# FFT filter and gated FFN on one core: three float32r passes in one first stage, another order of table loads, and matmuls on a cleared tile at the start

## The chip, the cores and the metric

The kernel runs on one core of one Trainium2 chip. The metric is device microseconds of that core for one execution, the median of several. The engines have short names in the profile: PE (TensorE matmul), PEld (its weight load), DVE (VectorE), ACT (ScalarE), POOL (GpSimd) and SP (SyncE, which here only issues DMAs).

## The reference

For 8 batches of 3136 rows by 256 columns, `x` is filtered in the frequency domain along its rows, and a gated feed-forward network with a depthwise convolution of three rows follows:

```python
X = np.fft.rfft(x, axis=1)
y = np.fft.irfft(X * (filt_r + 1j * filt_i)[None], n=x.shape[1], axis=1).astype(np.float32)
h = np.maximum(y @ w_in, 0.0)                       # 256 -> 1024
conv_out[s] = sum(conv_w[k] * h[s + k - 1] for k in range(3))
out = (h * sigmoid(conv_out)) @ w_out               # 1024 -> 256
```

## The kernel before, in words

The FFT of length 3136 = 112 x 28 is done as matmuls with tables. A batch is cut into 14 tiles of [112, 2, 256]; a tile goes through these steps, each named by its function:

- `load` (SP queue) brings a tile of `x` from DRAM.
- `first` is the first stage: float32 products of `x` with the 112x112 table `s1_sb`. For batches 0, 1, 3 and 5 it makes four products of 112 columns with the result turned (line 335), and `keep` copies them on ACT to the buffer `turn`; there are two of these. For batches 2, 4, 6 and 7 (`THROUGH_DRAM`) it makes two products of 256 columns (line 330), `keep` copies them on ACT to `ao` (line 341) and an ACT-queue DMA stores them to `a_dram`.
- The tile comes back in the other layout: `turn` (PE transposes, line 357) and `turned_rows` (an ACT copy to `a`, line 362), or `load_rows` (a DMA from `a_dram`).
- `second` (line 369) multiplies by the table `s2_sb` into `pp`. `filt` multiplies by the filter: three DVE products `u`, `v`, `v` that read `pp` in PSUM and a filter table in SBUF (lines 378 to 380), and one POOL sum `z` = `u` + `v` in SBUF (line 382).
- `third` (line 230) multiplies `z` by `i1_sb`, and `store` copies the result on ACT to `sb` (line 234) and stores it to `b_dram` by a DMA on the ACT queue.

A turn of the loop over i issues one step for each of several tiles: the first stage of tile i - 1, and, with m = i - 17, `second` of m - 1, `filt` of m - 2, `third` of m - 4. So a turn has `third`, `first`, `second` and perhaps `turn` on PE in that order. The order on each engine is that in which the code is written (`manual_schedule`). I call turns whose `first` belongs to batches 2, 4, 6, 7 *DRAM turns*, and those of batches 0, 1, 3, 5 *turned turns*. In turns whose tile m is of batches 0, 1, 3, 5 PE transposes too ("with transposes").

Two kinds of work run beside it. The tables `s2_sb`, `i1_sb` and the filter tables `t1_sb`, `t2_sb` come in seven pieces by POOL-queue DMAs (`load_filter`, at the turns of `FILTER_AT`; a small POOL copy `pace` holds each back until ACT has copied the tile before). The weights, stored as float64, are converted in eight slabs by a generator, `convert_weights`, from which each turn takes one step, or two: seven steps of a slab are DVE instructions on 128x512 words (`to_f32`, lines 150 to 162, behind the three products of the turn), the other three are a POOL sum, two ACT roundings to float32r and two POOL differences. Before, this runs from turn 36 at one step a turn, and two where i is a multiple of 8.

Then the FFN runs over 28 chunks of 896 rows. Its products are float32r, each in three passes on high and low parts (`mm3`, lines 167 to 169): the high part is the value rounded to float32r (`hi_act`), the low part what is left.

Of the kernel before, what the change touches and what calls it, by code (L numbers as in the profile page):

```python
# [19 lines left out]
G = 28  # L20
# [96 lines left out]
def tile_fft_filter_gated_ffn(  # L117
# [122 lines left out]
    xp = forward_pools.enter_context(tc.tile_pool(name="xp", bufs=1, side="right"))  # L240
    s1_sb = xp.tile([112, 112], F32, name="s1_sb")
    with (
        tc.tile_pool(name="fc", bufs=1) as fc,
# [23 lines left out]

        def load_filter(n, kept):
            b, k = kept
            nc.gpsimd.tensor_copy(pace, turns[turned_by[b] % 2][0:1, 0, 2 * k, 0:1])  # L270
            sl = slice(4 * n, 4 * n + 4)
            if n < 7:
                nc.gpsimd.dma_start(out=s2_sb[:, sl], in_=s2[:, sl])
                nc.gpsimd.dma_start(out=t2_sb[0:56, sl], in_=fi[0:56, sl])
                nc.gpsimd.dma_start(out=t1_sb[64:120, sl], in_=fr[64:120, sl])
            if n == 6:
                nc.gpsimd.dma_start(out=t1_sb[0:56, sl], in_=fr[0:56, sl])
            if n:
                sl = slice(4 * n - 4, 4 * n)
                nc.gpsimd.dma_start(out=i1_sb[:, sl], in_=i1[:, sl])  # L280

# [8 lines left out]
        def load_weights(k):  # L290
            raws[k] = raw = cv.tile([128, 2, 512], I32, name="raw")
            nc.sync.dma_start(out=raw, in_=w.rearrange("p (k t n) -> p k t n", t=2, n=512)[:, k])
# [6 lines left out]
        def convert_weights():  # L299

            for k in range(8):
                raw = raws.pop(k)
                em = cv.tile([128, 2, 512], I32, name="em", bufs=1)
                ws = cv.tile([128, 2, 256], F32, name="ws", bufs=1)
                yield from to_f32(ws.rearrange("p t n -> p (t n)"), raw.rearrange("p t n -> p (t n)"), em[:, 0], em[:, 1])
# [12 lines left out]

        def load(b, p):
            r = xp.tile([112, 2, D], F32, name="x", bufs=XBUFS)  # L320
            nc.sync.dma_start(out=r, in_=x[b].rearrange("(p n) d -> p n d", n=N2)[:, 2 * p:2 * p + 2])
            rows["x", b, p] = r

        def first(b, p):

            r = rows.pop(("x", b, p))
            if b in THROUGH_DRAM:
                ps = fps.tile([112, 2, D], F32, name="ps")
                for j in range(2):
                    nc.tensor.matmul(ps[:, j], lhsT=s1_sb, rhs=r[:, j], start=True, stop=True)  # L330
                return ps
# [55 lines left out]

        XBUFS = 6
# [10 lines left out]
        for i in range(XBUFS):  # L399
            load_first(i)  # L400
        csteps, wsteps = convert_conv(), convert_weights()
        done = NP * B + 1
        NI = done + LATE + N2 // 2 + 2
        END = NP * B - 4
        with tc.manual_schedule(engines=COMPUTE | {mybir.EngineType.SP}):
            for i in range(NI):
                m = i - SKEW
                if i == done:
# [3 lines left out]
                    yps.append(ctx.enter_context(tc.tile_pool(name="y_even", bufs=1, side="right", reuse_waits="tile")))  # L412
                if i:
                    load_first(i + XBUFS - 1)
                if i == 8:
# [26 lines left out]
                if pf is not None:  # L442
                    keep(*at(i - 1), pf)
                if i in FILTER_AT:
                    load_filter(FILTER_AT.index(i), at(i - 1))
                if pa is not None:
                    turned_rows(*at(m), pa)
                if 0 <= m - 1 < NP:
                    copy_filter(m - 1)
                if 14 <= i < 22:  # L450
# [125 lines left out]

THROUGH_DRAM = (2, 4, 6, 7)
PLAG = 6
PAUSE = (8,)
# [45 lines left out]
```

## Time and profile before

| what | value |
|---|---|
| median of 3 runs | 1535.78 us (1534.64 to 1537.65) |
| profiled execution, its time / its span | 1534.63 us / 1532.9 us |
| mean granted clock | 0.998 of full |
| PE busy in the span | 1511.3 us (99%) |
| DVE / ACT / POOL busy | 1285.1 / 1220.3 / 731.9 us |
| the loop's turns 29 to 112 (first stages of batches 2 to 7) | from 63.49 to 306.60 us |
| the FFN after the loop | from about 350 us |

The span is that of the profiled execution, and 1.7 us lie around it. Busy time says how long an engine had an instruction in it, not that the others waited for it; what sets the pace of a stretch is read from the distance of like instructions in order of time, and from what ended the idle time before them.

### The profile page before, as it was taken

The page shows a single profiled execution, that of the slowest core. Times are in us where ns is not written, and L with a number is a line of the kernel's source. Part 1 is how long each engine was busy: PE and PEld are TensorE (multiplying, and loading weights), DVE is VectorE, ACT ScalarE, POOL GpSimd, SP SyncE. Part 2 cuts the span into 40 slices and gives each one's busy share as a digit, 9 for nine tenths or more (in the row PEclk, how much of TensorE's full clock was granted, in tenths as well). Part 3 has the DMA queues.
Part 4 walks back from the last instruction along what each step waited for, and adds up shares of the span by engine and source line. Part 5 has one row for each costly group of instructions (what it writes and reads, how often), then busy time and mean ns, then how long its engine had stood idle before and what let it go on. Part 6 is the DMA issues. An engine that isn't in the chain of part 4 may idle for free.

```text
span 1532.9 us, 27503 instructions
## 1 busy us (share of the span) xinstructions
PE 1511.3 (99%) x10080; PEld 1420.1 (93%) x10080; DVE 1285.1 (84%) x1968; ACT 1220.3 (80%) x2227; POOL 731.9 (48%) x671
## 2 busy tenths in 40 slices
PE   7999999999999999999999999999999999999998
PEld 7888888888999999999999999999999999999998
DVE  2689898888888888888888888888888888888886
ACT  4664645567888888888888888888888888888886
POOL 5555566575444444444444444444444444444444
PEclk9999999999999999999999999999999999999999
DMA  8978797982111011111101111111011111000001
GB/s 219 274 238 287 235 285 244 317 254 76 52 55 37 25 43 55 43 49 49 49 31 43 49 48 32 55 49 43 25 55 49 49 44 54 19 25 25 25 25 49
DMA packets 105670, 141.07 MB, mean 92 GB/s; under 512 B 8813, under 2 KB 71773, under 8 KB 105536
## 3 DMA queue, kind: packets, MB, share of 16 engines
q1 hardware_dynamic: 76048, 95.01, 19.8%
q10 hardware_dynamic: 27392, 37.86, 8.1%
q0 software_dynamic: 2096, 6.45, 1.6%
q8 instruction: 80, 1.31, 0.3%
q14 instruction: 54, 0.44, 0.1%
HBM read 75.06 MB, written 64.23 MB: 91 GB/s over the span
## 4 chain that ended last, share of the span: by engine, by line
PE 94%; DMA 2%; ACT 1%; POOL 1%; DVE 1%; issue 1%; SPq 0%; ACTq 0%; POOLq 0%; DVEq 0%
PE ps_h L168 12%; PE ps_h L169 12%; PE po L520 12%; PE ps_h L167 12%; PE po L522 12%; PE po L521 12%; PE ps_h L207 6%; PE ps L230 5%; PE pp L369 5%; PE ps L330 3%; PE ps L335 3%; PE ps L357 1%; DMA i_sb<-in_i 1%; POOL z L382 1%; PE ps L207 1%
## 5 line engine op out<-in xcount | busy, mean ns | idle before, releaser
L142 POOL TENSOR_TENSOR g<-t,g 128x448 fp32r<-128x448 f32 x448 | 517.8, 1156 | 652.5 <-ACT g L136 258.0
L520 PE MATMUL po<-wo,g 128*128 128x256 f32 x1568 | 441.4, 281 | 0.0
L522 PE MATMUL po<-wo,g 128*128 128x256 f32 x1568 | 433.9, 277 | 0.0
L521 PE MATMUL po<-wo,g 128*128 128x256 f32 x1568 | 433.4, 276 | 0.0
L494 DVE SCALAR_TENSOR_TENSOR t<-ps_h,cw,t 128x448 f32<-128x448 f32 x448 | 305.9, 683 | 79.2 <-ACT t L489 67.9
L167 PE MATMUL ps_h<-y,wi 128*128 128x450 f32 x896 | 328.1, 366 | 1.3 <-DVE t L500 1.3
L168 PE MATMUL ps_h<-y,wi 128*128 128x450 f32 x896 | 328.8, 367 | 0.0
L169 PE MATMUL ps_h<-y,wi 128*128 128x450 f32 x896 | 328.2, 366 | 0.0
L495 DVE SCALAR_TENSOR_TENSOR t<-ps_h,cw,t 128x448 f32<-128x448 f32 x448 | 306.5, 684 | 16.0
L489 ACT ACTIVATE t<-ps_h,cw 128x448 f32<-128x448 f32 x448 | 285.4, 637 | 41.5 <-ACT ps_h L487 0.4
L520 PEld LDWEIGHTS po<-wo,g 128*128 128x128 f32 x1568 | 294.8, 188 | 7.1
L521 PEld LDWEIGHTS po<-wo,g 128*128 128x128 f32 x1568 | 294.3, 188 | 5.7
L522 PEld LDWEIGHTS po<-wo,g 128*128 128x128 f32 x1568 | 294.5, 188 | 0.2 <-POOL g L142 0.2
L500 DVE TENSOR_TENSOR t<-ps_h,t 128x448 f32<-128x448 f32 x448 | 275.4, 615 | 0.1
L487 ACT ACTIVATE ps_h<-ps_h 128x450 f32<-128x450 f32 x448 | 251.9, 562 | 26.6 <-PE ps_h L169 22.0
L499 ACT ACTIVATE t<-t 128x448 f32<-128x448 f32 x448 | 255.1, 569 | 14.2 <-DVE t L495 12.4
L136 ACT ACTIVATE g<-t 128x448 fp32r<-128x448 f32 x448 | 254.7, 568 | 0.2 <-DVE t L500 0.2
L382 POOL TENSOR_TENSOR z<-u,v 120x512 f32<-120x512 f32 x112 | 156.8, 1401 | 125.9 <-DVE v L380 97.1
L169 PEld LDWEIGHTS ps_h<-y,wi 128*128 128x128 f32 x896 | 167.9, 187 | 14.0
L167 PEld LDWEIGHTS ps_h<-y,wi 128*128 128x128 f32 x896 | 169.6, 189 | 8.4 <-DVE t L500 1.8
L168 PEld LDWEIGHTS ps_h<-y,wi 128*128 128x128 f32 x896 | 167.9, 187 | 6.7
L139 DVE TENSOR_TENSOR y<-ps_h,y 128x448 fp32r<-128x448 f32 x98 | 103.7, 1058 | 71.1 <-ACT y L136 71.1
(69 smaller groups left out, 1616.1 us busy)
## 6 DMA issues: line engine op xcount, KB each, us to landing
x<-in_x SPq DMA_DIRECT2D x112, 224.0 KB, 3.6
b_dram<-sb ACTq DMA_DIRECT2D x109, 224.0 KB, 3.5
out<-ot SPq DMA_DIRECT2D x27, 896.0 KB, 4.1
br<-b_dram SPq DMA_DIRECT2D x98, 224.0 KB, 2.6
a_dram<-ao ACTq DMA_DIRECT2D x56, 224.0 KB, 3.2
a<-a_dram SPq DMA_DIRECT2D x56, 224.0 KB, 4.1
raw<-in_w SPq DMA_DIRECT2D x8, 512.0 KB, 5.5
turn<-b_dram SPq DMA_DIRECT2D x14, 224.0 KB, 4.7
```

What stands on the lines that cost most here:

```text
L142: nc.gpsimd.tensor_tensor(out=dst, in0=src, in1=hi.bitcast(F32), op=ALU.subtract)
L167: nc.tensor.matmul(ps, lhsT=wh, rhs=rh, start=start, stop=False, **kw)
L168: nc.tensor.matmul(ps, lhsT=wh, rhs=rl, start=False, stop=False, **kw)
L169: nc.tensor.matmul(ps, lhsT=wl, rhs=rh, start=False, stop=stop, **kw)
L489: nc.scalar.activation(t, h[:, 1:SUB + 1], AF.Copy, scale=cw[:, 1, f:f + 1])
L494: nc.vector.scalar_tensor_tensor(out=t, in0=h[:, 0:SUB], scalar=cw[:, 0, f:f + 1], in1=t, op0=ALU.mult, op1=ALU.add)
L495: nc.vector.scalar_tensor_tensor(out=t, in0=h[:, 2:SUB + 2], scalar=cw[:, 2, f:f + 1], in1=t, op0=ALU.mult, op1=ALU.add)
L499: nc.scalar.activation(t, t, AF.Sigmoid)
L500: nc.vector.tensor_mul(t, h[:, 1:SUB + 1], t)
L520: nc.tensor.matmul(o, lhsT=gh[:, sl], rhs=wo[0][:, f], start=first, stop=False, skip_group_check=True)
L521: nc.tensor.matmul(o, lhsT=gh[:, sl], rhs=wo[1][:, f], start=False, stop=False, skip_group_check=True)
L522: nc.tensor.matmul(o, lhsT=gl[:, sl], rhs=wo[0][:, f], start=False, stop=last, skip_group_check=True)
```

## The change

Three things are changed, all before the FFN.

1. In DRAM turns the first stage becomes three float32r passes over the 512 columns of a tile: `s1` and `x` are split into high and low parts. In each such turn this adds one ACT instruction (`split_high`, 512 columns), one POOL difference (384 columns) ahead of the sum `z`, and one DVE difference (`BY_DVE` = 128 columns) behind the three products of `filt`. Two float32 products of 256 columns go, three float32r products of 512 come. There are 56 such turns.
2. The steps of the weight conversion are dealt out by a credit from turn 32 on: 0.75 a DRAM turn, 1.5 a turned turn. Only one raw slab is held, and the next is loaded when the slab before is through its DVE steps. Buffers for `x` go from 6 to 4 after the first 18 tiles; the first 18 lie in the part of `t2_sb` that is filled last.
3. The tables come in the order of `TABLES` (turns for `s2`, the filter and `i1` of each piece). DVE clears `eye_sb`, and 12 products of 128 columns on it stand ahead of PE's first product.

```diff
+    s1_parts = [xp.tile([112, 112], F32R, name=f"s1{h}") for h in range(2)]
...
-            raws[k] = raw = cv.tile([128, 2, 512], I32, name="raw")
+            raws[k] = raw = cv.tile([128, 2, 512], I32, name="raw", bufs=1)
...
+                if k < 7:
+                    load_weights(k + 1)
...
-                if k < 6:
-                    load_weights(k + 2)
...
-            r = xp.tile([112, 2, D], F32, name="x", bufs=XBUFS)
+            n = b * NP + p
+            if n < AHEAD * 3:
+                at = 2 * (n % AHEAD) + G - 2 - 2 * AHEAD
+                r = t2_sb[0:112, at:at + 2]
+            else:
+                r = xp.tile([112, 2, D], F32, name="x", bufs=4)
...
+        def split_high(b, p):
+            h = xp.tile([112, 2, D], F32R, name="xh", bufs=2)
+            hi_act(h, rows["x", b, p])
+            rows["xh", b, p] = h
+
+        def split_low(b, p):
+            r, h = rows["x", b, p], rows["xh", b, p]
+            t = xp.tile([112, 2, D], F32R, name="xl", bufs=2)
+            r, h, lo = (t.rearrange("p n d -> p (n d)") for t in (r, h, t))
+            rows["xl", b, p] = t
+            sl = slice(BY_DVE, 2 * D)
+            lo_pool(lo[:, sl], r[:, sl], h[:, sl])
+            yield
+            sl = slice(0, BY_DVE)
+            lo_dve(lo[:, sl], r[:, sl], h[:, sl])
...
-                for j in range(2):
-                    nc.tensor.matmul(ps[:, j], lhsT=s1_sb, rhs=r[:, j], start=True, stop=True)
+                mm3(ps, *s1_parts, rows.pop(("xh", b, p)), rows.pop(("xl", b, p)))
...
-        FILTER_AT = (12, 15, 18, 20, 22, 24, 26, 28)
...
+            for k in range(WARM):
+                nc.tensor.matmul(pw[:, 0:128], lhsT=eye_sb, rhs=eye_sb, start=True, stop=True)
...
+                low = iter(())
+                if (bp := at(i)) and bp[0] in THROUGH_DRAM:
+                    split_high(*bp)
+                    low = split_low(*bp)
+                next(low, None)
                 if bp := at(m - 2):
                     filt(*bp)
+                next(low, None)
...
-                if i in (28, 34):
-                    load_weights((i - 28) // 6)
-                if i >= 36:
-                    for _ in range(2 if i % 8 == 0 else 1):
+                if i == 28:
+                    load_weights(0)
+                if i >= 32:
+                    credit += 0.75 if (bp := at(i)) and bp[0] in THROUGH_DRAM else 1.5
+                    for _ in range(int(credit)):
+                        credit -= 1
                         next(wsteps, None)
...
+TABLES = (
+    (0, 9, 11, 14),
+    (1, 13, 15, 17),
...
+WARM = 12
+BY_DVE = 128
+AHEAD = 6
```

Three engines' orders follow, at the places that matter. `v_105` to `v_108` are the two buffers of `v`, `em`, `ws` and `raw` the conversion's words, `xh` and `xl` the high and low part of a tile of `x`.

DVE in DRAM turns of batch 4, before: the three products of a turn, and behind them at most a conversion step.

```order
L378 TENSOR_TENSOR u<-pp,t_sb 120x512
L379 TENSOR_TENSOR v_105<-pp,t_sb 56x512
L380 TENSOR_TENSOR v_105<-pp,t_sb 56x512
L156 TENSOR_SCALAR em<-raw 128x512
L378 TENSOR_TENSOR u<-pp,t_sb 120x512
L379 TENSOR_TENSOR v_106<-pp,t_sb 56x512
L380 TENSOR_TENSOR v_106<-pp,t_sb 56x512
L158 SCALAR_TENSOR_TENSOR ws<-em 128x512
```

And DVE in DRAM turns of batch 4 of the changed kernel:

```order
L400 TENSOR_TENSOR u<-pp,t_sb 120x512
L401 TENSOR_TENSOR v_108<-pp,t_sb 56x512
L402 TENSOR_TENSOR v_108<-pp,t_sb 56x512
L139 TENSOR_TENSOR xl<-x,xh 112x128
L152 TENSOR_SCALAR em<-raw 128x512
L400 TENSOR_TENSOR u<-pp,t_sb 120x512
L401 TENSOR_TENSOR v_107<-pp,t_sb 56x512
L402 TENSOR_TENSOR v_107<-pp,t_sb 56x512
L139 TENSOR_TENSOR xl<-x,xh 112x128
L154 TENSOR_TENSOR em<-em 128x512
```

The low part stands between the products and the conversion step, so a turn has two instructions on SBUF operands alone where it had one. Counted over the whole order, seven turns of each of the batches 2, 4, 6 and 7 have both.

DVE in turned turns of batch 3 of the changed kernel, where the credit deals out two steps every other turn:

```order
L400 TENSOR_TENSOR u<-pp,t_sb 120x512
L401 TENSOR_TENSOR v_107<-pp,t_sb 56x512
L402 TENSOR_TENSOR v_107<-pp,t_sb 56x512
L154 TENSOR_TENSOR em<-em 128x512
L400 TENSOR_TENSOR u<-pp,t_sb 120x512
L401 TENSOR_TENSOR v_108<-pp,t_sb 56x512
L402 TENSOR_TENSOR v_108<-pp,t_sb 56x512
L156 TENSOR_SCALAR em<-raw 128x512
L158 SCALAR_TENSOR_TENSOR em<-em 128x512
```

Two DVE steps stand together in four turns of batch 3 and in four of batch 5; before, there were five such turns in the whole loop.

ACT in a DRAM turn with transposes, before (`DMA` rows are issues on its queue):

```order
L234 ACTIVATE sb<-ps 112x512
L236 DMA b_dram_62<-sb 112x512
L341 ACTIVATE ao<-ps 112x512
L342 DMA a_dram_57<-ao 112x2x256
L362 ACTIVATE a<-ps 112x512
```

ACT in such a turn of the changed kernel:

```order
L136 ACTIVATE xh<-x 112x512
L234 ACTIVATE sb<-ps 112x512
L236 DMA b_dram_62<-sb 112x512
L363 ACTIVATE ao<-ps 112x512
L364 DMA a_dram_57<-ao 112x2x256
L384 ACTIVATE a<-ps 112x512
```

The rounding of the next tile's high part stands between `a` of one turn and `sb` of the next; nothing else of ACT's turn moved.

POOL's first table loads, before:

```order
L270 COPY pace<-turn_102 1x1
L273 DMA s_sb<-in_s 112x480
L274 DMA t_sb<-in_fi 56x1024
L275 DMA t_sb<-in_fr 56x1024
L270 COPY pace<-turn_101 1x1
L273 DMA s_sb<-in_s 112x480
L274 DMA t_sb<-in_fi 56x1024
L275 DMA t_sb<-in_fr 56x1024
L280 DMA i_sb<-in_i 120x448
```

And those of the changed kernel:

```order
L271 COPY pace<-turn_104 1x1
L275 DMA s_sb<-in_s 112x480
L271 COPY pace<-turn_104 1x1
L279 DMA t_sb<-in_fi 56x1024
L280 DMA t_sb<-in_fr 56x1024
L271 COPY pace<-turn_104 1x1
L275 DMA s_sb<-in_s 112x480
L271 COPY pace<-turn_104 1x1
L277 DMA i_sb<-in_i 120x448
L271 COPY pace<-turn_103 1x1
L279 DMA t_sb<-in_fi 56x1024
L280 DMA t_sb<-in_fr 56x1024
```

The first piece of `i1` (`i_sb`) stood behind two pieces of the filter; now it stands behind one, and the first load is asked for at turn 9 and no longer at turn 12.

## Rows read from the trace of the kernel before

**Rows 1.** The page's chain that ended last, by engine.

```profile
PE 94%; DMA 2%; ACT 1%; POOL 1%; DVE 1%; issue 1%; SPq 0%; ACTq 0%; POOLq 0%; DVEq 0%
```

**Rows 2.** Busy time of each engine by stretch: length, engines, clock, DMA share, GB/s.

```profile
20.00:34.00 14.00, 10.34 (x76) 9.55 (x76) 5.99 (x10) 7.98 (x14) 6.69 (x13) 1.00 1.02 243
34.00:41.00 7.00, 5.47 (x18) 4.55 (x19) 4.01 (x7) 1.14 (x2) 5.19 (x8) 0.51 0.96 226
63.49:108.54 45.05, 43.24 (x225) 35.91 (x224) 34.24 (x52) 27.17 (x46) 19.44 (x15) 1.00 0.84 260
108.54:147.10 38.56, 38.02 (x234) 33.35 (x232) 34.56 (x51) 18.51 (x35) 24.52 (x21) 1.00 0.86 268
147.10:189.91 42.81, 41.82 (x217) 35.19 (x216) 37.92 (x56) 24.49 (x43) 25.18 (x19) 1.00 0.79 247
189.91:227.59 37.68, 37.68 (x234) 33.40 (x233) 35.41 (x53) 18.24 (x34) 23.32 (x19) 1.00 0.90 281
227.59:306.60 79.01, 79.01 (x397) 66.18 (x396) 68.04 (x102) 43.26 (x76) 48.62 (x38) 1.00 0.88 280
```

**Rows 3.** PE in order of time: start, length, line; DRAM turns with and without transposes.

```profile
87.31 1.03 PE L330 MATMUL ps<-x,s_sb 112*112 112x256 f32 x4
88.18 1.03 PE L369 MATMUL pp<-a,s_sb 112*120 112x256 f32 x4
90.35 1.03 PE L330 MATMUL ps<-x,s_sb 112*112 112x256 f32 x4
...
283.26 1.03 PE L330 MATMUL ps<-x,s_sb 112*112 112x256 f32 x4
285.85 1.03 PE L330 MATMUL ps<-x,s_sb 112*112 112x256 f32 x4
```

**Rows 4.** PE in order of time, two float32r passes of the FFN.

```profile
702.18 0.36 PE L168 MATMUL ps_h<-y,wi 128*128 128x450 f32 x1
702.38 0.37 PE L169 MATMUL ps_h<-y,wi 128*128 128x450 f32 x1
```

**Rows 5.** DVE in order of time, turns with one conversion step.

```profile
87.72 0.69 DVE L380 TENSOR_TENSOR v<-pp,t_sb 56x512 f32<-56x512 f32 x1
...
204.32 0.69 DVE L378 TENSOR_TENSOR u<-pp,t_sb 120x512 f32<-120x512 f32 x1
...
206.44 0.43 DVE L160 TENSOR_SCALAR em<-ws 128x512 int32<-128x512 int32 x1
206.90 0.69 DVE L378 TENSOR_TENSOR u<-pp,t_sb 120x512 f32<-120x512 f32 x1
```

**Rows 6.** DVE in order of time, a turn with two conversion steps.

```profile
169.09 0.69 DVE L380 TENSOR_TENSOR v<-pp,t_sb 56x512 f32<-56x512 f32 x1
169.81 0.43 DVE L152 TENSOR_SCALAR em<-raw 128x512 int32<-128x512 int32 x1
170.28 1.64 DVE L154 TENSOR_TENSOR em<-em 128x512 int32<-128x512 int32 x1
171.95 0.69 DVE L378 TENSOR_TENSOR u<-pp,t_sb 120x512 f32<-120x512 f32 x1
```

**Rows 7.** POOL in order of time, the sum in that turn.

```profile
169.95 1.42 POOL L382 TENSOR_TENSOR z<-u,v 120x512 f32<-120x512 f32 x1 [1.61 <-DVE v L380]
```

**Rows 8.** A source line's instructions: count, shortest, median and longest in ns, first and last.

```profile
L160 DVE TENSOR_SCALAR em<-ws x8: 427/427/1383, 101.3 to 282.5; 128x512 int32<-128x512 int32 x8
```

**Rows 9.** ACT in order of time, a DRAM turn in which it catches up.

```profile
78.34 0.60 ACT L362 ACTIVATE a<-ps 112x512 f32<-112x512 f32 x1 [0.40 <-PE ps L230]
78.83 0.59 ACT L234 ACTIVATE sb<-ps 112x512 f32<-112x512 f32 x1
...
80.86 0.60 ACT L362 ACTIVATE a<-ps 112x512 f32<-112x512 f32 x1 [0.40 <-PE ps L357]
```

**Rows 10.** The page's groups: the FFN's rounding to float32r.

```profile
L136 ACT ACTIVATE g<-t 128x448 fp32r<-128x448 f32 x448 | 254.7, 568 | 0.2 <-DVE t L500 0.2
```

**Rows 11.** Groups by shape up to 345 us: a float32r low part on POOL.

```profile
L142 POOL TENSOR_TENSOR wi<-ws,wi 128x256 fp32r<-128x256 f32 x8 | 5.8, 728 | 0.0
```

**Rows 12.** PE in order of time, the first product with `i1`.

```profile
35.52 2.02 PE L230 MATMUL ps<-z,i_sb 120*112 120x256 f32 x4 [3.71 <-DMA i_sb<-in_i]
```

More of the change, by code (lines that the diff above doesn't have):

```diff
@@ L266, in tile_fft_filter_gated_ffn, with load_tables @@
         turned_by = {b: n + 1 for n, b in enumerate(b for b in range(B) if b not in THROUGH_DRAM)}
-        def load_filter(n, kept):
+        def load_tables(names, kept):
             b, k = kept
             nc.gpsimd.tensor_copy(pace, turns[turned_by[b] % 2][0:1, 0, 2 * k, 0:1])
[L271 to L280, printed above, removed]
+            for name, n in names:
+                sl = slice(4 * n, 4 * n + 4)
+                if name == "s2":
+                    nc.gpsimd.dma_start(out=s2_sb[:, sl], in_=s2[:, sl])
+                elif name == "i1":
+                    nc.gpsimd.dma_start(out=i1_sb[:, sl], in_=i1[:, sl])
+                else:
+                    nc.gpsimd.dma_start(out=t2_sb[0:56, sl], in_=fi[0:56, sl])
+                    nc.gpsimd.dma_start(out=t1_sb[64:120, sl], in_=fr[64:120, sl])
+                    if n == 6:
+                        nc.gpsimd.dma_start(out=t1_sb[0:56, sl], in_=fr[0:56, sl])
         def copy_filter(p):
@@ L303, in convert_weights @@
                 em = cv.tile([128, 2, 512], I32, name="em", bufs=1)
-                ws = cv.tile([128, 2, 256], F32, name="ws", bufs=1)
-                yield from to_f32(ws.rearrange("p t n -> p (t n)"), raw.rearrange("p t n -> p (t n)"), em[:, 0], em[:, 1])
+                yield from to_f32(em[:, 1].bitcast(F32), raw.rearrange("p t n -> p (t n)"), em[:, 0], em[:, 1])
+                if k < 7:
+                    load_weights(k + 1)
+                ws = em[:, 1].bitcast(F32).rearrange("p (t n) -> p t n", t=2)
                 yield
@@ L386, in at @@
             return divmod(i, NP) if 0 <= i < NP * B else None
-        XBUFS = 6
         ABUFS = 4
-        FILTER_AT = (12, 15, 18, 20, 22, 24, 26, 28)
+        TABLES_AT = {}
+        for n, at_s2, at_f, at_i1 in TABLES:
+            for name, i in (("s2", at_s2), ("f", at_f), ("i1", at_i1)):
+                TABLES_AT.setdefault(i, []).append((name, n))
         SKEW = NP + 3
@@ L398, in tile_fft_filter_gated_ffn @@
         nc.sync.dma_start(out=s1_sb, in_=s1)
-        for i in range(XBUFS):
+        for i in range(AHEAD):
             load_first(i)
         csteps, wsteps = convert_conv(), convert_weights()
+        credit = 0.0
         done = NP * B + 1
@@ L404, in tile_fft_filter_gated_ffn @@
         END = NP * B - 4
+        nc.vector.memset(eye_sb, 0.0)
         with tc.manual_schedule(engines=COMPUTE | {mybir.EngineType.SP}):
+            pw = fps.tile([128, 512], F32, name="ps")
+            for k in range(WARM):
+                nc.tensor.matmul(pw[:, 0:128], lhsT=eye_sb, rhs=eye_sb, start=True, stop=True)
             for i in range(NI):
@@ L412, in tile_fft_filter_gated_ffn @@
                     yps.append(ctx.enter_context(tc.tile_pool(name="y_even", bufs=1, side="right", reuse_waits="tile")))
-                if i:
-                    load_first(i + XBUFS - 1)
+                if 2 <= i < 3 * AHEAD:
+                    load_first(i + AHEAD - 2)
+                elif i > 3 * AHEAD:
+                    load_first(i + 3)
                 if i == 8:
@@ L443, in tile_fft_filter_gated_ffn @@
                     keep(*at(i - 1), pf)
[L444 to L445 removed]
+                if i in TABLES_AT:
+                    load_tables(TABLES_AT[i], at(i - 1))
                 if pa is not None:
@@ L577 @@
 THROUGH_DRAM = (2, 4, 6, 7)
+TABLES = (
+    (0, 9, 11, 14),
+    (1, 13, 15, 17),
+    (2, 17, 18, 19),
+    (3, 19, 20, 21),
+    (4, 21, 22, 23),
+    (5, 23, 24, 25),
+    (6, 25, 26, 27),
+)
+WARM = 12
+BY_DVE = 128
+AHEAD = 6
 PLAG = 6
```

4 lines of the change are left out of this document (added).

## The prediction, as put on record

> **What bounds the kernel now.** I read the chain that ended last first: PE is 94% of it [rows 1], so time is gained or lost where PE is made faster or made to wait. Then busy time by stretch: turns 29 to 112 of the loop, which hold the change, take 45.05 + 38.56 + 42.81 + 37.68 + 79.01 = 243.1 us, and PE is busy in 239.8 of these at the full granted clock [rows 2]. DVE comes next: 34.24 + 34.56 + 37.92 + 35.41 + 68.04 = 210.2 us. So PE sets the pace, and DVE has 33 us to spare in the whole stretch, but only 2.3 of 37.68 in batch 5. In order of time a DRAM turn with transposes takes PE 3.04 us and one without 2.59, of which the first stage, from its start to that of `second`, is 0.87 [rows 3]. Behind turn 112 nothing is changed but places in memory, so the FFN stays as it is.
>
> **The first stage on PE.** Two passes of 450 columns in the FFN stand 0.20 us apart [rows 4]. For 512 columns that is 0.23, and 0.70 for three. 0.70 in place of 0.87 takes 0.17 us off each of 56 DRAM turns: 9.5 us if PE stays the bound. It can't get less than that from PE alone; whether it gets any of it is for the other engines to say.
>
> **ACT.** The DRAM turn gains a rounding of 512 columns. Where ACT catches up, a whole turn from `a` to `a`, both DMA issues within it, takes it 80.86 - 78.34 = 2.52 us [rows 9]. The rounding of 448 columns lasts 0.568 [rows 10], so 0.65 for 512; in that catching up an instruction of 0.60 is followed by the next after 0.49 [rows 9], so the rounding adds 0.53 (bounds 0.49 and 0.65). ACT's turn is 3.05 with transposes, where PE's was 3.04, and 2.56 without, where PE's was 2.59. So the turns with transposes, 38 of the 56, can't get faster at all, and the 9.5 us shrink to nearly nothing before DVE is looked at.
>
> **DVE, without waits.** From `u` to the conversion step a turn takes 206.44 - 204.32 = 2.12 us, and a short step another 0.46 [rows 5]; a long one (line 154) lasts 0.69 undisturbed against 0.43, so 0.72. Turns 28 to 111 are 84: 84 x 2.12 = 178.1. The eight slabs have 32 short and 24 long steps: 32.0. The new low parts, 56 of 128 columns, have no row. They cost more than nothing and less than a short step of 512 columns (0.46); I take 0.25: 14.0. Sum 224.1, or 2.67 a turn: under the 243.1.
>
> **DVE, with waits for POOL.** Here lies the cost. In a turn with one step, `z` on POOL starts 0.14 to 0.17 us behind the last product, while the step runs. In a turn with two, the first step starts at 169.81, `z` at 169.95, and the second step, begun at 170.28, lasts 1.64 us in place of 0.69, to 171.92 [rows 6]; `z` ends at 171.37 [rows 7]. It does nothing until the sum is through. The same happens to a short step: 1.383 us at worst, 0.427 at the median of eight [rows 8]. The delay is 0.95 us in both. So the second of two DVE instructions on SBUF operands in one turn pays about 0.95 us, because POOL's sum comes between; the products `u` and `v`, which read PSUM, don't wait.
>
> The Trainium skill, "SBUF — State Buffer", section "Who interferes with whom", says that a DVE instruction with two SBUF inputs, or in its two-port modes, and a GpSimd instruction that reads SBUF lock each other out, the one that starts first for its whole length. The trace agrees for the steps (1.64 against 0.69). It has no 128-column difference of `x` and `xh`; by the page that has two SBUF inputs and takes the lock too, and then all the turns counted next would wait, 36 us in the sum; if it took no lock, only the 8 of the turned turns would, 7.6 us.
>
> The order puts the new low part right behind the products and the step behind it. The low part is short, so `z` arrives while it runs and has POOL before the step. That is 7 turns in each of batches 2, 4, 6 and 7, 28 in all. With 1.5 steps a turned turn, 4 turns of batch 3 and 4 of batch 5 have two DVE steps. Two turns of batch 2 have the low part and a copy of the filter table. Together 38, at 0.95: 36.1 us. The bounds are 7.6 (only the pairs of steps wait, as in rows 6) and 36.1 plus whatever the low part itself waits for POOL's low part. I take the full 36.1, since the low part is like line 154, a difference of two SBUF tensors, which does wait.
>
> DVE's sum is then 224.1 + 36.1 = 260.2 us against 243.1. By batch it is the same picture: a DRAM batch has 14 x 2.12 + 14 x 0.25 + 4.0 + 7 x 0.95 = 43.8, a turned one 29.7 + 8.0 + 3.8 = 41.5, where PE took 37.7 to 38.6 for a turned one and 79.0 for batches 6 and 7 together. Each turn's `z` is needed by `third` two turns on, and each low part by `first` of the next turn; DVE's products of a turn end at 88.41 [rows 5], and the product that would need the low part starts at 90.35 [rows 3], so with 0.25 for the low part DVE may fall behind by 1.7 us before PE waits. That is saved once: 258.5, 15.4 us more than before.
>
> **POOL.** The low part of 384 columns, at 0.728 for 256 [rows 11], is 1.09 us. In batches 6 and 7 POOL goes from 48.6 [rows 2] to 48.6 + 28 x 1.09 = 79.1, as much as the 79.0 us of that stretch; DVE's 87.6 covers it.
>
> **The early part.** PE stands 3.71 us at its first product with `i1` [rows 12], and then the granted clock is 0.51 from 34 to 41 us, the lower level of 1.2 GHz, behind that idle time; 5.47 us of PE work there [rows 2] would have taken half, so 2.7 us more. Asking for `i1` earlier can give at most 3.71 + 2.7 = 6.4 us. At least it gives nothing, because the DMA engines are full in that stretch (1.02 and 0.96 busy [rows 2]) and the bytes are the same. But two tiles of `x` less are loaded ahead, 448 KB, 1.9 us at the 243 GB/s of that stretch, and the first tables are asked for three turns earlier. I take 4 us. The 12 products on the cleared tile run while the first `x` is on its way; what they win at the very start the full DMA takes back by turn 20: 0. The single raw slab is loaded about two turns before its first step: 0, but see below.
>
> **The sum.** 15.4 - 4 = 11.4 us on the profiled execution's own time of 1534.63 (span 1532.9 and 1.7 around it; 1.1 us below the median): 1546.
>
> **Rivals.**
>
> *ACT is the bound, the low part does not let POOL in* (faster). If the step follows the low part closely enough to keep POOL waiting, as the first of two steps does, the 28 + 2 waits vanish: DVE has 231.7 us and the DRAM turns go by ACT, 3.05 or 2.56, no change. Turned batches at 41.5 against 38.6 and 37.7 lose about 1 us each beyond DVE's lead, and the stalls of before behind the pairs give as much back. Only the 4 us of the early part remain: 1530.6. Point of decision: whether steps behind a low part last 0.43 and 0.69 or 1.3 and more. Against it: POOL got between two steps that followed each other by 0.47 us. Chance 0.20.
>
> *Part of the waits* (no change). If a third to a half of those 30 turns escape, the waits are 26.6 to 21.9 us and DVE needs 249.0 to 244.3: with the early 4 us off, 1536.5 to 1531.8. Chance 0.14.
>
> *PE stays the bound* (the change does what it says): -9.5 - 4, 1521. It needs ACT at 2.85 a turn, where rows 9 and 10 give 3.05. Chance 0.05.
>
> *Worse than forecast.* The low part on DVE and that on POOL are freed by the same rounding, so each can wait for the other too: up to 1.09 us in the 28 DRAM turns without a step, of which DVE's lag hides most; and a step that waits for its only raw slab holds the products behind it. Half of 28 x 1.09 on top: 1561. Chance 0.06.
>
> **How the numbers follow.** The forecast, DVE bound with waits in most of the 28 turns, has 0.55, and spans 1540 (early gain of 6.4, four of the waits escaped) to 1556 (early gain 0, low part at 0.35, half way to its upper bound). A measurement of this kernel can tell about 0.2%, 3.1 us, from no change. Faster: 0.20 + 0.05 = 0.25. Same: 0.14. Slower: 0.55 + 0.06 = 0.61. The range reaches from 1528 (the ACT rival, with 2.6 us more of the early part) to 1556; outside lie the PE rival, part of the ACT rival, and the worst case.
>
> **What the profile would show.** Right: conversion steps in DRAM turns of 1.3 us and more, DVE without idle time there, PE waiting at `third` for `z` and at `first` for `xl`, stretches of some 44 us for a DRAM batch and 41 for a turned one. First product with `i1` some 4 us earlier, and no stretch at the lower clock. Wrong: steps of 0.43 and 0.69 behind the low parts and turns of 3.05 and 2.56 set by ACT; or PE without idle time at 2.87 a turn.

## The result, and the profile after

The changed kernel takes 1550.34 us (median of 4 runs, 1549.8 to 1552.02) against 1535.21 for the kernel before: a ratio of 1.0102, 95% interval 1.009 to 1.0114. It is slower, by 15.1 us.

The page of the changed kernel: span, busy time by engine, and the chain that ended last.

```profile
span 1550.2 us, 27712 instructions
PE 1514.9 (98%) x10048; PEld 1409.6 (91%) x10048; DVE 1325.4 (85%) x2026; ACT 1245.8 (80%) x2284; POOL 793.7 (51%) x735
PE 85%; DVE 6%; POOL 2%; issue 2%; ACT 2%; DMA 1%; ACTq 0%; POOLq 0%; DVEq 0%; SPq 0%
```

DVE's share of the chain is 6%, where it was 1% [rows 1]. Then the stretches of the changed kernel that answer to [rows 2] (batches 2, 3, 4, 5, and 6 with 7), and the two early ones: length, engines, clock, DMA share, GB/s.

```profile
20.00:34.00 14.00, 12.42 (x90) 11.38 (x90) 6.98 (x12) 8.58 (x15) 8.21 (x17) 1.00 1.02 233
34.00:41.00 7.00, 6.75 (x44) 5.92 (x43) 6.57 (x11) 5.19 (x9) 5.82 (x10) 1.00 1.01 273
...
57.51:105.78 48.27, 43.49 (x212) 34.24 (x211) 46.28 (x67) 33.36 (x60) 35.45 (x29) 0.96 0.79 238
105.78:150.88 45.10, 40.50 (x234) 34.37 (x232) 39.80 (x57) 18.91 (x36) 25.50 (x21) 0.96 0.78 243
150.88:195.61 44.73, 41.23 (x204) 31.99 (x203) 42.57 (x65) 30.18 (x56) 39.26 (x34) 1.00 0.78 232
195.61:240.04 44.43, 38.93 (x234) 32.91 (x232) 39.87 (x57) 18.93 (x36) 24.79 (x21) 1.00 0.77 236
240.04:326.40 86.36, 80.11 (x374) 59.73 (x373) 82.58 (x127) 56.15 (x102) 77.23 (x64) 1.00 0.87 270
```

The early part gains: the first DRAM first stage comes at 57.51 us instead of 63.49, and the clock from 34 to 41 us is 1.00 instead of 0.51. Behind it every stretch loses: 3.2, 6.5, 1.9, 6.8 and 7.4 us. PE now stands idle 3.5 to 6.3 us in each stretch, in the turned batches (the second and the fourth) too, whose first stage is not changed.

Several kinds of row say why. First DVE and POOL of the changed kernel in order of time, in a DRAM turn of batch 2 and one of batch 4, the latter with the product of PE that waits; then the low part on DVE as a source line.

```profile
83.74 0.29 DVE L139 TENSOR_TENSOR xl<-x,xh 112x128 fp32r<-112x128 f32 x1
83.78 2.00 POOL L404 TENSOR_TENSOR z<-u,v 120x512 f32<-120x512 f32 x1
83.95 0.68 DVE L154 TENSOR_TENSOR em<-em 128x512 int32<-128x512 int32 x1
...
171.22 1.01 POOL L142 TENSOR_TENSOR xl<-x,xh 112x384 fp32r<-112x384 f32 x1 [0.52 <-ACT xh L136]
171.75 1.86 DVE L139 TENSOR_TENSOR xl<-x,xh 112x128 fp32r<-112x128 f32 x1
172.18 1.28 POOL L404 TENSOR_TENSOR z<-u,v 120x512 f32<-120x512 f32 x1
173.53 0.41 DVE L156 TENSOR_SCALAR em<-raw 128x512 int32<-128x512 int32 x1
173.75 0.46 PE L168 MATMUL ps<-xl,s 112*112 112x512 f32 x1 [0.41 <-DVE xl L139]
```

```profile
L139 DVE TENSOR_TENSOR xl<-x,xh x56: 291/293/2831, 57.7 to 321.9; 112x128 fp32r<-112x128 f32 x56
```

At 83.74 the low part takes 0.29 us and the step behind it its plain 0.68; POOL's sum is the one that waits (2.00 us for 1.28). At 171.75 it is the low part that waits: POOL's own low part, freed by the same rounding, was first; the low part on DVE lasts until POOL is through with it and with the sum, and PE waits for it. The median of the 56 is 0.293 us, but eleven are over 1 us, and added up they take 36.5 us where 56 plain ones would take 16.4: some 20 us of waiting, on the low part and not on the step behind it. Of the 28 steps that stand behind a low part, 27 last 0.41 to 0.69 us, which is their time without a wait.

Then DVE of the changed kernel in the turned batch 3, in order of time.

```profile
117.29 0.43 DVE L156 TENSOR_SCALAR em<-raw 128x512 int32<-128x512 int32 x1
117.75 1.64 DVE L158 SCALAR_TENSOR_TENSOR em<-em 128x512 f32<-128x512 int32 x1
119.42 0.69 DVE L400 TENSOR_TENSOR u<-pp,t_sb 120x512 f32<-120x512 f32 x1
...
132.02 0.43 DVE L150 TENSOR_SCALAR em<-raw 128x512 int32<-128x512 int32 x1 [2.84 <-POOL wo L142]
```

The second step of a pair waits as in [rows 6]. There are eight pairs; in two of them it is the first step that waits (1.48 us for 0.43). The other row is a wait that was not there before. The change also writes a slab's result into the second half of `em` (line 306) and drops the tile `ws`, so the first step of a slab must wait until POOL has made the low parts of the slab before out of the same tile: 2.84 us twice, 6.4 us in all. POOL makes them behind its sum, and that behind DVE's products. PE feels this wait as a late `z`. Two rows of PE, the first in batch 2, where it waits for the first `xl`, the second in batch 3, behind that wait of DVE:

```profile
60.68 0.46 PE L168 MATMUL ps<-xl,s 112*112 112x512 f32 x1 [2.58 <-DVE xl L139]
136.24 1.93 PE L230 MATMUL ps<-z,i_sb 120*112 120x256 f32 x4 [2.10 <-POOL z L404]
```

Behind each of the two the granted clock is at its lower level (0.50, 1.2 GHz) for 3.4 us, from 61.3 and from 136.4; this is the 0.96 of the two stretches above. PE was busy all through both, so each cost it about 1.7 us (an estimate: half of the 3.4 us); what of this reaches the end was not tried.

Last, PE and ACT in DRAM turns of batch 6.

```profile
254.86 0.60 ACT L384 ACTIVATE a<-ps 112x512 f32<-112x512 f32 x1 [0.40 <-PE ps L379]
255.15 0.59 PE L167 MATMUL ps<-xh,s 112*112 112x512 f32 x1
257.91 0.60 ACT L384 ACTIVATE a<-ps 112x512 f32<-112x512 f32 x1 [0.40 <-ACT ao L363]
258.01 0.58 PE L167 MATMUL ps<-xh,s 112*112 112x512 f32 x1
260.88 0.58 PE L167 MATMUL ps<-xh,s 112*112 112x512 f32 x1
260.96 0.60 ACT L384 ACTIVATE a<-ps 112x512 f32<-112x512 f32 x1 [0.40 <-ACT ao L363]
264.00 0.60 ACT L384 ACTIVATE a<-ps 112x512 f32<-112x512 f32 x1 [0.40 <-ACT ao L363]
264.65 0.50 PEld L391 LDWEIGHTS pp<-a,s_sb 112*120 112x120 f32 x3 [0.32 <-ACT a L384]
```

PE makes its turns in 2.86 and 2.87 us, 0.17 or 0.18 under the 3.04 of [rows 3], while ACT goes from `a` to `a` in 3.05. PE can do so for a few turns, after it was held up; then it waits for `a`.

### The profile page after: what moved, and what is told of

It is laid out like the page before. It is cut to its first block, busy times and chain, and to the rows that moved or that the text cites. A ratio compares the mean times of both kernels' runs of the same rounds, so it can differ in the third digit from the quotient of the medians.

```text
span 1550.2 us, 27712 instructions
## 1 busy us (share of the span) xinstructions
PE 1514.9 (98%) x10048; PEld 1409.6 (91%) x10048; DVE 1325.4 (85%) x2026; ACT 1245.8 (80%) x2284; POOL 793.7 (51%) x735
## 4 chain that ended last, share of the span: by engine, by line
PE 85%; DVE 6%; POOL 2%; issue 2%; ACT 2%; DMA 1%; ACTq 0%; POOLq 0%; DVEq 0%; SPq 0%
PE ps_h L168 12%; PE ps_h L169 12%; PE po L562 12%; PE ps_h L167 12%; PE po L564 11%; PE po L563 11%; PE ps_h L207 6%; PE pp L391 3%; PE ps L230 3%; DVE v L401 1%; DVE u L400 1%; DVE v L402 1%; PE ps L357 1%; POOL z L404 1%; DVE xl L139 1%
## 5 line engine op out<-in xcount | busy, mean ns | idle before, releaser
L404 POOL TENSOR_TENSOR z<-u,v 120x512 f32<-120x512 f32 x112 | 162.7, 1453 | 72.3 <-DVE v L402 41.9
```

## The experiments

In each run I read, from PE in order of time, when the first and the last product of the first stage of a DRAM batch start, and lay the times between them side by side: from the first to the last within batch 2, 4, and 6 with 7 ("DRAM"), and from the last of one to the first of the next over the turned batches 3 and 5 ("turned"). These times are of one profiled execution each; sums are of the unrounded times. The ratios have their 95% intervals.

| kernel | begin | DRAM | turned | end | median us, ratio to before |
|---|---|---|---|---|---|
| before | 63.49 | 42.0 + 39.8 + 76.4 = 158.2 | 41.6 + 40.7 = 82.3 | 304.01 | 1535.2 |
| changed | 57.51 | 45.1 + 41.5 + 81.9 = 168.5 | 48.3 + 47.7 = 95.9 | 321.93 | 1550.3, 1.0102 (1.009 to 1.0114) |
| early part only | 57.41 | 157.2 | 82.3 | 296.91 | 1529.8, 0.997 (0.9955 to 0.9984) |
| tables only | 59.13 | 158.7 | 82.3 | 300.13 | 1532.5, 0.9978 (0.9967 to 0.9989) |
| early, no cleared tile | 58.50 | 158.6 | 82.3 | 299.40 | 1531.7, 0.9978 (0.9969 to 0.9988) |
| float32 first stage | 57.16 | 156.5 | 95.3 | 309.03 | 1541.4, 1.0043 (1.0027 to 1.0059) |
| no low parts | 56.24 | 158.1 | 95.4 | 309.74 | 1546.8, 1.0068 (1.0051 to 1.0086) |
| low part on DVE alone | 57.75 | 161.3 | 96.4 | 315.44 | 1547.3, 1.0073 (1.0057 to 1.0088) |
| low part on POOL alone | 57.16 | 165.4 | 96.6 | 319.14 | 1551.5, 1.0107 (1.0089 to 1.0125) |
| DVE's low part from PSUM | 57.83 | 165.0 | 95.6 | 318.49 | 1548.6, 1.0091 (1.0076 to 1.0106) |
| own `ws` | 57.75 | 169.9 | 93.4 | 320.96 | 1550.5, 1.0099 (1.0077 to 1.0122) |
| steps spread | 56.30 | 167.4 | 89.9 | 313.63 | 1546.9, 1.0078 (1.0061 to 1.0095) |
| one step a turn | 57.83 | 167.1 | 82.3 | 307.24 | 1540.0, 1.0034 (1.0023 to 1.0045) |
| built from the parts | 57.74 | 165.5 | 83.7 | 306.92 | 1538.5, 1.0019 (1.0006 to 1.0032) |

### The parts apart: early part, and first stage

The early part put into the kernel before:

```diff
-        XBUFS = 6
...
-        FILTER_AT = (12, 15, 18, 20, 22, 24, 26, 28)
...
-                if i:
-                    load_first(i + XBUFS - 1)
+                if 2 <= i < 3 * AHEAD:
+                    load_first(i + AHEAD - 2)
+                elif i > 3 * AHEAD:
+                    load_first(i + 3)
...
+TABLES = (
+    (0, 9, 11, 14),
+    (1, 13, 15, 17),
...
+WARM = 12
+AHEAD = 6
```

> The kernel before with only the early part of the change: tables in the order of need, x of the first batch ahead in the place of t2_sb, 12 products on the cleared tile. First stage in float32, steps, raw and ws as before. Theory (the early part is worth the 6.0 us by which the changed kernel reaches its first DRAM first stage earlier, and all the loss lies behind it): 1529 us, first DRAM first stage at 57.5 instead of 63.5, batches 2 to 7 as in rows 2. Rival (the early gain is given back when the tables' loads collide with later work): 1533 to 1536.

It came out so: 1529.8, the batches as before. Of the 7.1 us by which the last first stage is earlier, 2.9 are lost behind it: from there to the FFN's first product it takes 49.6 us instead of 46.75, since PE waits 2.03 us for the fourth group of last-stage products, whose tile of batch 0 is not yet loaded, and behind this wait the granted clock is 0.50 for 3.4 us from 310.2. PE of this kernel there, in order of time:

```profile
308.65 1.12 PE L207 MATMUL ps<-m_sb,turn 112*128 112x112 f32 x8 [2.03 <-DMA turn<-b_dram]
```

Then two smaller parts of it. The first is the kernel of the early part without the products on the cleared tile (the edit below); the second is the kernel before with `TABLES` alone, so with its ring of six `x` tiles and without the place in `t2_sb`:

```diff
-WARM = 12
+WARM = 0
```

> The kernel before with the early part of the change but without the 12 products on the cleared tile. Theory (the early gain is the tables' order, and the products give nothing, since the DMA engines are full until turn 20): 1530, within 1.5 us of the 1529.8 with the products, and the same first DRAM first stage at 57.4. Rival (the products save a start at the lower clock): 1531 to 1534.

> The kernel before with only the tables in the order of need; x in its ring of six tiles and no products on the cleared tile. Theory (the wait for the first table i1 of 3.71 us and the lower clock behind it are the early gain): no wait for i1 over 1 us, no stretch at the lower clock, 1529 to 1531. Rival (part of the gain comes from the x tiles of the first batch, which are loaded later there): 1532 to 1535.

Both came out in the span of their rivals, at 1531.7 and 1532.5. Where DRAM work begins, in one execution each, the tables give 4.4 us of the 6.1; it is 58.50 without the products and 57.41 with them, which would make these worth 1.1 there, and `x` in `t2_sb` 0.6. But the eleven kernels of the table that have the whole early part differ by 1.6 among themselves, from 56.24 to 57.83, so one execution each does not settle these two shares. With the tables alone no wait for `i1` is left, but PE waits for `x`, as that rival had it, and the granted clock is 0.50 for 3.4 us behind this wait, from 22.4. PE of this kernel, in order of time:

```profile
21.19 4.31 PE L336 MATMUL ps<-s_sb,x 112*128 112x112 f32 x24 [1.96 <-DMA x<-in_x]
```

In the medians the three kernels differ by 0.8 to 2.7 us and their intervals overlap; the whole early part takes 5.7 us off the kernel before, the tables alone 2.5. So the tables by themselves make the kernel faster and bring most of the earlier start of the DRAM work; what the other two parts add to the time is not shown.

The changed kernel with its first stage in float32 again:

```diff
-                mm3(ps, *s1_parts, rows.pop(("xh", b, p)), rows.pop(("xl", b, p)))
+                for j in range(2):
+                    nc.tensor.matmul(ps[:, j], lhsT=s1_sb, rhs=r[:, j], start=True, stop=True)
...
-                    split_high(*bp)
-                    low = split_low(*bp)
+                    pass
```

> The changed kernel with the first stage of the DRAM batches on float32 again, without the rounding and the two low parts; early part, 0.75 and 1.5 steps a turn, single raw slab and sum in em are kept. Theory (in the DRAM batches the low part on DVE, 36.6 us with its waits, is the loss): stretches of the DRAM batches back at the time of before (45.1, 42.8 and 79.0 us) or a little less, since they hold fewer steps; the turned batches stay at 42 to 45 us instead of 38, because the pairs of steps and the wait for em are kept; 1533 to 1543, about 1538. Rival (the pace of the steps and the wait for em are most of the loss in the DRAM batches too): 1545 or more.

The theory held: the DRAM batches are back (156.5), and the turned ones stay at 95.3, 13.0 over before (47.9 for batch 3 here is 44.9 counted as in [rows 2], where 41.6 is 38.56). So 13.0 of the 23.9 us that DRAM and turned batches lose together have nothing to do with the first stage.

### The steps in the turned batches

Own tile for the slab's result:

```diff
-                yield from to_f32(em[:, 1].bitcast(F32), raw.rearrange("p t n -> p (t n)"), em[:, 0], em[:, 1])
+                ws = cv.tile([128, 2, 256], F32, name="ws", bufs=1)
+                yield from to_f32(ws.rearrange("p t n -> p (t n)"), raw.rearrange("p t n -> p (t n)"), em[:, 0], em[:, 1])
...
-                ws = em[:, 1].bitcast(F32).rearrange("p (t n) -> p t n", t=2)
```

> The changed kernel with the step's result in a tile of its own, ws, as before (room from the pad and from the tile of the convolution weights). Theory (the first step of a slab waits for POOL's low part of the slab before because both lie in em: 6.4 us in four waits, and half clock behind one of them): no step of line 150 lasts or waits over 2 us, no stretch at the lower clock, 1544 to 1547. Rival (DVE has the work behind these waits to do anyway, and waits elsewhere): 1549 to 1551.

The time is the rival's. The wait for POOL is gone, and so is the lower clock in batch 3; the turned batches take 2.5 us less, the DRAM ones 1.4 more, and the time is the same. In this one execution the lower clock in batch 2 lasted 6.8 us in place of 3.4, so part of the 1.4 may be chance. The wait is real, but taking it away alone did not make the kernel faster.

The same number of steps, but the first of two between the products `v`:

```diff
             nc.vector.tensor_mul(v[64:120], pp[0:56], t2_sb[0:56, sl])
+            if between is not None:
+                next(between, None)
             nc.vector.tensor_mul(v[0:56], pp[64:120], t2_sb[64:120, sl])
...
+                if nsteps == 2 and nstep % 10 < 7:
+                    between = wsteps
+                    nsteps -= 1
...
                 if bp := at(m - 2):
-                    filt(*bp)
+                    filt(*bp, between)
```

> The changed kernel with the same 1.5 steps a turned turn, but where a turn has two DVE steps, the first of them stands between the two products v instead of behind the last, so that no two DVE instructions on SBUF operands follow each other and POOL's sum of the turn before has ended. Theory (the turned batches lose their 6.7 us each because the second of a pair waits about 0.95 us for the sum): no second step of 1.4 us and more in a turned turn, last to first first stage over a turned batch 41.5 to 44 us instead of 48.3 and 47.7, 1541 to 1545. Rival (1.5 steps a turn are too much for DVE by themselves, 2.12 and 0.6 us against PE's 2.6): 46 us or more for a turned batch, 1548 to 1551.

Between the theory and its rival. DVE of this kernel in batch 3, in order of time:

```profile
115.48 0.43 DVE L156 TENSOR_SCALAR em<-raw 128x512 int32<-128x512 int32 x1
115.94 0.69 DVE L404 TENSOR_TENSOR v<-pp,t_sb 56x512 f32<-56x512 f32 x1
116.66 0.69 DVE L158 SCALAR_TENSOR_TENSOR em<-em 128x512 f32<-128x512 int32 x1
```

No step of a pair waits any more (0.43 and 0.69), and the turned batches fall by 6.0 us, to 89.9. Of the 7.6 us still above before, the wait for POOL behind `em` could be most: the waits list has 7.6 us for it in this run, and the lower clock is there for 3.4 us in each of the two turned batches. That is not tried apart.

One step in every turn:

```diff
-                    credit += 0.75 if (bp := at(i)) and bp[0] in THROUGH_DRAM else 1.5
-                    for _ in range(int(credit)):
-                        credit -= 1
-                        next(wsteps, None)
+                    next(wsteps, None)
```

> The changed kernel with one step in every turn from turn 32 on, in DRAM and turned batches alike, so no pairs. Theory (pairs cost the turned batches 6.7 us each, while a single step behind a low part in a DRAM batch does not wait): turned batches 41 to 42.5 us, DRAM batches 1 to 2 us longer each by the steps moved to them, 1541 to 1546. Rival (what DVE has to do and to wait in sum stays the same, only its place changes): 1548 to 1552.

The theory held, and by a little more than I gave it: the turned batches are exactly as before, 82.3, and the DRAM batches with more steps in them are not longer in sum (167.1 for 168.5). The result still goes into `em`, but at this pace the waits for POOL behind it come to 1.8 us in place of 6.4, and the granted clock never falls in the loop. So this edit takes away the pairs and most of the wait for `em` at once. By itself it takes 10.3 us off the changed kernel.

### The first stage in the DRAM batches

Without both low parts (the second pass reads `xh` again):

```diff
-                mm3(ps, *s1_parts, rows.pop(("xh", b, p)), rows.pop(("xl", b, p)))
+                h = rows.pop(("xh", b, p))
+                mm3(ps, *s1_parts, h, h)
...
-                    low = split_low(*bp)
```

> The changed kernel without the two low parts: ACT still rounds x, and the second of the three passes reads the rounded x once more, so PE and ACT do all of their work and DVE and POOL none of the new. The first stage then leaves out the low part of x. Theory (PE would gain its 0.17 us a turn if DVE and POOL let it, and ACT is not the bound): from the first to the last first stage 39.6 us in batch 2, 36.3 in batch 4 and 71.6 in batches 6 and 7, against 41.8, 38.5 and 76.2 with the float32 first stage at the same pace of steps; 1532, that is 9.5 under the 1541.4 of that kernel. Rival (ACT with its 3.05 and 2.56 us a turn is the bound): the stretches of the float32 first stage, 1541.

The rival was right in the DRAM batches, which gain nothing: 158.1 against 156.5 with float32. ACT and PE of this kernel in batch 2, in order of time:

```profile
75.00 0.59 PE L167 MATMUL ps<-xh,s 112*112 112x512 f32 x1
75.32 0.60 ACT L385 ACTIVATE a<-ps 112x512 f32<-112x512 f32 x1 [0.40 <-ACT ao L364]
75.97 0.71 PEld L392 LDWEIGHTS pp<-a,s_sb 112*120 112x120 f32 x4 [0.36 <-ACT a L385]
...
78.05 0.58 PE L167 MATMUL ps<-xh,s 112*112 112x512 f32 x1
78.36 0.60 ACT L385 ACTIVATE a<-ps 112x512 f32<-112x512 f32 x1 [0.40 <-ACT ao L364]
79.01 0.72 PEld L392 LDWEIGHTS pp<-a,s_sb 112*120 112x120 f32 x4 [0.37 <-ACT a L385]
```

PE's turn is ACT's 3.04 to 3.05, and in each PE waits 0.36 us for `a` before its weights can be loaded. So ACT takes the 9.5 us of PE away by itself, before DVE and POOL are asked. The median is 5.4 us above that of the float32 kernel. In the profiled execution 4.3 us of this lie behind these batches: `turn<-b_dram` is waited for 3.2 us there, and the products behind that wait run at the lower clock (granted 0.50 from 322.5 to 327 us; 2.02 us for the 1.12 of other runs):

```profile
322.56 2.02 PE L207 MATMUL ps<-m_sb,turn 112*128 112x112 f32 x8 [3.19 <-DMA turn<-b_dram]
```

DVE's 128 columns alone:

```diff
+        xls = [xp.tile([112, 2, D], F32R, name=f"xl{k}") for k in range(2)]
+        for t in xls:
+            nc.gpsimd.memset(t.bitcast(F32), 0.0)
...
-            t = xp.tile([112, 2, D], F32R, name="xl", bufs=2)
+            t = xls[p % 2]
...
-            sl = slice(BY_DVE, 2 * D)
-            lo_pool(lo[:, sl], r[:, sl], h[:, sl])
```

> The changed kernel with the low part of DVE's 128 columns alone; the 384 columns of POOL are zero all along and POOL does nothing new, so the first stage leaves out the low part of these columns. Theory (POOL's low part, which holds up SBUF for 1.0 us more a turn, makes DVE wait; DVE's own 0.25 us a turn is small): no low part over 1 us unless behind the sum, DRAM batches 1 to 3 us above the kernel without low parts, 1532 to 1539. Rival 1 (DVE's work alone is too much): within 3 us of the changed kernel, 1547 to 1550. Rival 2 (the sum z alone makes DVE wait as much as the low part and the sum did): 56 low parts with a mean of 0.6 us, as in the changed kernel, 1545 or more.

The DRAM batches take 161.3 us, 3.2 over the kernel without low parts, as the theory had it, and the changed kernel 7.2 more; so two thirds of what the low parts cost there is POOL's share. But the median, 1547.3, is in rival 1's span: the theory's 1532 to 1539 left out that this kernel too keeps the turned batches at 96.4. The longest low part is 1.42 us:

```profile
L139 DVE TENSOR_TENSOR xl<-x,xh x56: 291/293/1416, 57.8 to 315.4; 112x128 fp32r<-112x128 f32 x56
```

All 512 columns on POOL:

```diff
-            sl = slice(0, BY_DVE)
-            lo_dve(lo[:, sl], r[:, sl], h[:, sl])
...
-BY_DVE = 128
+BY_DVE = 0
```

> The changed kernel with all 512 columns of the low part on POOL, none on DVE. POOL's low part is then about 1.3 to 1.45 us and with its sum of 1.3 to 1.4 about 2.8 a turn. Theory (the wait of the low part on DVE for the one on POOL is the loss): DVE loses 36.6 us of work, the DRAM batches go by POOL at 2.8 to 2.9 a turn, 40 us each, and the time is 1538 to 1544. Rival (POOL becomes the bound, and its longer low part now holds the steps on DVE too): DRAM batches at 44 us or more, 1549 to 1556.

The rival's time, though not its batches of 44 us (42.8, 40.9, 81.7). DVE has less to do, but now its steps wait. DVE and POOL of this kernel in batch 4, in order of time:

```profile
168.31 1.27 POOL L142 TENSOR_TENSOR xl<-x,xh 112x512 fp32r<-112x512 f32 x1 [0.49 <-ACT xh L136]
168.53 2.57 DVE L156 TENSOR_SCALAR em<-raw 128x512 int32<-128x512 int32 x1
169.53 1.28 POOL L402 TENSOR_TENSOR z<-u,v 120x512 f32<-120x512 f32 x1
```

Is it POOL's hold on SBUF that keeps the low part, or its data? One operand from PSUM instead:

```diff
-            lo_dve(lo[:, sl], r[:, sl], h[:, sl])
+            lo_dve(lo[:, sl], last_pp[0][0:112, 0, sl], h[:, sl])
...
             pp, v = psums.pop((b, p)), turned[p % 2]
+            last_pp[:] = [pp]
```

> The changed kernel, but the low part on DVE subtracts from a piece of the second stage's PSUM tile instead of x, so 128 columns of the low part hold other numbers; columns, waits and order stay. Theory (it is POOL's hold on SBUF that keeps the low part on DVE, as it has two SBUF operands, and the products on PSUM never wait): all 56 low parts last 0.2 to 0.35 us, their sum falls from 36.6 to about 16, and the DRAM batches get 2 to 3 us shorter each, unless the step behind is held in its place: 1540 to 1547. Rival 1 (POOL then holds the step behind the low part instead): steps of 2 us and more in DRAM turns, 1548 to 1551. Rival 2 (the low part waits for its data, not for POOL's hold): long low parts as before, 1550.

The low part as a source line of this kernel:

```profile
L139 DVE TENSOR_TENSOR xl<-pp,xh x56: 291/292/294, 58.0 to 317.8; 112x128 fp32r<-112x128 f32 x56
```

All 56 take 0.29 us, though they still need the rounding's result: it was the hold. The Trainium skill, "SBUF — State Buffer", section "Who interferes with whom", has the lock for a DVE instruction with two SBUF inputs; this agrees with 2.83 us at most with two and 0.294 with one. Yet the DRAM batches gain only 3.5 us, and the time 1.7, which the intervals of the two ratios do not tell from nothing: of the fourteen steps in batches 6 and 7, six now last 1.2 to 2.35 us, as rival 1 said. The wait goes over to the next DVE instruction on SBUF.

### A kernel from the parts that looked good

Early part, float32 in batches 2 and 4, three passes in 6 and 7 with 192 columns on DVE, own `ws`, at most one DVE step a turn from turn 32 to 96:

```diff
+                if b in SPLIT:
+                    mm3(ps, *s1_parts, rows.pop(("xh", b, p)), rows.pop(("xl", b, p)))
+                    return ps
...
+                    for _ in range(3 if nstep % 10 == 8 else 1):
+                        nstep += 1
+                        next(wsteps, None)
...
-BY_DVE = 128
+SPLIT = (6, 7)
+BY_DVE = 192
```

> Made of the parts that look good: early part as changed, float32 first stage in batches 2 and 4, three passes in 6 and 7 with 192 columns of the low part on DVE, ws a tile of its own, and never more than one DVE step a turn, from turn 32 to turn 96. Theory (without pairs, and with few steps beside the low parts, PE sets the pace in batches 6 and 7 too): 0.17 us off some 20 of the 28 turns, 1524 to 1528 against 1529.8 for the early part alone. Rival (sum and low parts of a turn alone take as long as PE's turn): batches 6 and 7 no shorter than 76.4 us from the first to the last first stage, 1529 to 1533.

A miss, worse than its rival: batches 6 and 7 take 83.6 us instead of 76.4, and half of this is lost in batch 7, where no steps are left. One row of DVE there:

```profile
279.88 2.12 DVE L139 TENSOR_TENSOR xl<-x,xh 112x192 fp32r<-112x192 f32 x1
```

The low part waits for POOL here without any step beside it. But only two of the 28 low parts last over 1 us, and what all of them wait comes to 3.7 us; where the rest of the 7.2 us goes is not shown.

Three versions beat both kernels: the early part alone, the same without the cleared tile, and the tables alone.

## Why the prediction was right, and where it was not

The time (1546 predicted, in 1528 to 1556) and the direction were right, and three of the steps stand.

- **ACT.** 3.05 us a turn with transposes was forecast; the changed kernel has 3.05, and the kernel without low parts shows that this cancels the 9.5 us of PE: the DRAM batches get 1.6 us longer, not 9.5 shorter. (The trace of before has 40 turns with transposes among the 56, not 38; nothing hangs on it.)
- **Pairs of steps.** Eight were counted at 0.95 us each, 7.6. The first one waits 0.95 (1.64 for 0.69), and with a product between the two the wait is gone.
- **DVE as the bound of the DRAM batches**, with PE waiting for `z` and for `xl`: 46.3 busy of 48.3 us in batch 2, 42.6 of 44.7 in batch 4, 82.6 of 86.4 in batches 6 and 7 (waits within an instruction counted as busy), and that is how the rows read.

The step that failed is the one with the largest term: that POOL's sum gets in between the low part and the step behind it, 28 turns at 0.95 us, with the low part like line 154. All but one of these 28 steps last 0.41 to 0.69. By the point of decision that I set for the ACT rival it should have been that rival's 1530.6. What stood in its place is what I had only as the case "worse": the low part on DVE waits for POOL's, which the same rounding frees, and for the sum behind it. The runs price it, first to last first stage: 4.2 us for DVE's 128 columns over the kernel without low parts (315.44 - 57.75 less 309.74 - 56.24), 6.7 more for POOL's 384, which I had set aside as covered by DVE's work.

The terms that were mis-sized:

- **Turned batches.** 41.5 us each were forecast, 45.1 and 44.4 came: 13.3 over before, not 6.8. I added up DVE's time and took PE for able to catch up. But with one step DVE's turn is 2.59 us (from 119.42 to the next `u` at 122.01), and PE's only 0.1 more (37.68 us for 14 in [rows 2] is 2.69), so little of a pair's wait is made good; and I didn't see that the slab's result in `em` makes the next slab wait (6.4 us), with the lower clock behind one of these waits.
- **Early part.** 6.0 us instead of 4, within its bounds. The first `i1` product comes 3.6 us earlier, at 31.88, with no lower clock there, as said. That the products on the cleared tile give nothing is neither shown nor refuted: the one execution without them began 0.7 us behind the latest with them.
- **The low part itself.** 0.29 us instead of 0.25: 16.4 us for the 56 instead of 14.0.

So DRAM and turned batches gave 10.3 and 13.6 us more from the first to the last first stage, 23.9 in all, less 6.0 for the early part and 0.6 in the FFN: 17.3 between the two spans (1550.2 and 1532.9), while the medians differ by 15.1. The sum was right to 4.3 us, and that is in good part luck: the waits forecast behind the low parts, 26.6 us, did not come, and those on the low parts and for `em`, 20 and 6.4 us, came to nearly the same. Nor was DVE's time the whole time: the five stretches took 268.9 us, and DVE was busy in 251.1 of them.

What stays open: how a wait of DVE for POOL is shared between low part, step and sum in a given turn; each edit that freed one brought part of the wait to another. And what the turned batches' 13 us owe to the pairs, to `em` and to the lower clock one by one: spreading the pairs gave 6.0 back, a tile of its own for the result 2.5, one step a turn all of it.

## What to carry to other kernels

Count a turn's work on every engine before giving one engine less of it: PE's 0.17 us a turn was gone as soon as ACT had one more instruction in it. A DVE instruction on SBUF operands can wait for the POOL work on SBUF of the same turn: here the second of two conversion steps waited 0.95 us for the sum, and a low part up to 2.5 us for POOL's low part and the sum. An instruction on PSUM between two steps took their wait away; freeing the low part alone only moved its wait to the step behind. And side work should be dealt out evenly where the bound engine has no turn in which to catch up: one step a turn instead of 0.75 and 1.5 was worth 10 us here.

## What was not expected of the hardware

A DVE instruction right behind the 128-column low part kept POOL out, while one behind a step of 512 columns did not. At 83.95 the step starts 0.08 us before the low part's record ends; at 170.28 the second step starts 0.04 us after the end of the first [rows 6], and POOL's sum has come in between. That the overlap makes the difference is argued from these rows, not tried. And work that comes earlier can meet a load that is not there yet: PE waited up to 3.2 us for `b_dram`, with products at the lower clock behind it.
